# Neighbourhood attention: sixteen border stores spread over later steps and two queues

## The chip, the cores and the metric

The kernel runs on one core of one Trainium2 chip. The metric is the device time of one execution in microseconds (us). Runs of the same kernel are summed up by their median.

## The reference

The input is an image of 224 x 224 pixels with 192 channels (bf16). Each pixel attends to a 7 x 7 neighbourhood with dilation 2: the neighbours of one pixel all have its row parity and its column parity, and near the border the window is shifted inwards, not cut.

```python
q, k, v = split(x @ wqkv)                       # 192 channels each
r0 = clip(row - 6, 0, 224 - 13); c0 = clip(col - 6, 0, 224 - 13)
neighbours = (r0 + 0,2,..,12) x (c0 + 0,2,..,12)  # 49 pixels
p = softmax(q . k[neighbours] * 192**-0.5)
out = (p @ v[neighbours]) @ wo
```

## The kernel before, in words

**Tiles and steps.** Rows of one parity `rc` are taken eight at a time (`BR`), so the image makes 28 steps, listed in `seq` (L491): step 0 and step 1 work on even rows, then odd and even rows alternate. The loop over steps is at L522 with index `si`. A step has T = 7 rounds `t`, and in every round TensorE computes one group of scores (`s_group`, L399 and L400), which ScalarE turns into exponentials (L403). The query side of the next step is prepared in rounds 0 to 2 (`g_piece`, L343 and L351; evacuated by ScalarE and VectorE, L355 to L365), and edge columns are prepared by `edge_item` (L287, then VectorE's copies L295) and copied into place by `edge_copies`, half of them on GpSimd (POOL, L322 and L323).

**Values.** `y_unit` (L405) multiplies the exponentials with the input itself: for each column tile n it reads the key block in `XN[rc]`, which holds 14 tiles of 128 rows, in two halves that take turns as the steps advance down the image. The plan `yplan` (L379) says in which round each of the four units of a step begins; units of a step reach into rounds 0 and 1 of the next step. The unit of round 2 (cc = 0, h = 1) reads tiles 7 to 13, in that order; that of round 4 (cc = 0, h = 0) starts with tile 0.

**Output.** In rounds 3 to 6 the products of the step before are finished: `o_mm` (L436) applies the folded output weights, VectorE divides by the sums (L440, L451) and writes into the buffer `o_sb`, of which there are three in turn (L442). After round 6, `store` (L453) sends the finished buffer of the step before to memory from the SP queue (L596). For eight rows at a constant distance that is five transfers: one large one for the middle of the rows and four small ones for the sides. Step 0 has the image's upper border in it and its eight rows are not evenly spaced (1, 3, 5 and 0, 2, 4, 6, 8): it takes eight transfers of one row each and two times four small ones, sixteen in all.

**Loads.** In step `si` the key block that step `si` + 1 is the first to use is loaded into `XN` by fourteen transfers, one for each tile: tiles 12 and 11 from SP in round 0 (L570), tiles 10, 9 and 8 from POOL in round 0 (L571) and the remaining nine, 13 and then 7 down to 0, from POOL in round 1 (L573). A load waits until TensorE has read the old contents of its tile for the last time. The transposed loads `xt` (L91) are issued from SP in rounds 1 and 4. VectorE builds masks in round 2 of steps 1, 2, 3 and 8 (`masks`, L593; instructions at L187 and L188).

**What sets the order.** The schedule is manual: each engine and each queue works through its instructions in the order in which the program writes them. A transfer waits on its issuing queue, and everything behind it on that queue waits too. On SP, and likewise on POOL, a transfer also waits for the transfer eight before it on that queue to have landed.

Of the kernel before, what the change touches and what calls it, by code (L numbers as in the profile page):

```python
# [7 lines left out]
BF = mybir.dt.bfloat16  # L8
# [14 lines left out]
NO = 7  # L23
# [4 lines left out]
def kernel(  # L28
# [7 lines left out]
    nc = tc.nc  # L36
    B, H, W, C = x.shape
# [14 lines left out]
    work = ctx.enter_context(tc.tile_pool(name="work", bufs=3))  # L52
# [181 lines left out]
    for reg in (LO, HI, OLO, OHI):  # L234
        c0, cn, p0 = reg
        pool_, tag = ((ps_s, "s"), (ps_y, "y"))[reg in (OLO, OHI)]
# [27 lines left out]
    def key_copy(rc, m, cc, ea, eb):  # L264
        if not 0 <= m < NJ:
            return
        t, k0 = xt[m], 64 * (m % 2)
        v, d = "p r (n c) -> p r n c", DROW[cc]
        ea(out=XA[rc][:, cc, :, k0:k0 + 64].rearrange("p n (r c) -> p r n c", c=KC),  # L269
                       in_=t[:, 2 * cc, rc:16:2, :].rearrange(v, c=KC))  # L270
        eb(out=XB[cc][rc][d, :, k0:k0 + 64].rearrange("p n (r c) -> p r n c", c=KC),  # L271
                       in_=t[d, 1, rc:16:2, :].rearrange(v, c=KC))
# [25 lines left out]
    def step_rows(rc, j):  # L298
        if rc == 0:
            first = (0, 3, j - 1, 10) if j > 0 else (0, 3, 0, 1)  # L300
            return [first, (3, 5, j, 0)]
        last = (5, 3, j + 1, 1) if j < NJ - 1 else (5, 3, j, 10)
        return [(0, 5, j, 7), last]
# [122 lines left out]
    def o_mm(st, ns, ccs=(0, 1), home=None):  # L426

        if home is None:
            po = ps_go.tile([128, 4, 256], F32, name="po", tag="go")
        else:  # L430
            po = home[0].tile([128, 2, 256], F32, name="po" + home[1], tag=home[1])
        k = 0
        for n in ns:
            for cc in ccs:
                for kt in range(2):
                    nc.tensor.matmul(po[:, k, 0:C + 1], lhsT=st.ysb[cc][:, kt, n, :], rhs=WP[:, cc, kt, :],  # L436
                                     start=(kt == 0), stop=(kt == 1))
                k += 1
        rs = work.tile([128, 4, 1], F32, name="rs", tag="rs", bufs=4)
        nc.vector.reciprocal(out=rs[:, 0:k], in_=po[:, 0:k, C:C + 1])  # L440
        if st.o is None:
            st.o = work.tile([128, 2 * NO, C], BF, name="o_sb", tag="o_sb", bufs=3)  # L442
        t0, step = 2 * ns[0] + ccs[0], 3 - len(ccs)
        return po, rs, k, st.o[:, t0:t0 + step * (k - 1) + 1:step, :]

# [4 lines left out]
            return  # L450
        nc.vector.tensor_tensor(out=o, in0=po[:, 0:k, 0:C], in1=rs[:, 0:k].to_broadcast([128, k, C]), op=ALU.mult)  # L451

    def store(st, engs, parts=None, cols=None):  # L453

        o = st.o
        n0, n1 = cols or (0, NO)
        runs = _affine([16 * b + l0 + 2 * i for (r0, n_, b, l0) in step_rows(st.rc, st.j) for i in range(n_)])
        q = [0]

        def dma(**kw):  # L460
            engs[q[0] % len(engs)].dma_start(**kw)
            q[0] += 1
        for (i0, n_, d0, stp) in runs:
            rows = slice(d0, d0 + (n_ - 1) * stp + 1, stp)
            if parts is not None and cols is None:
                pass
            elif n_ == BR:
                dma(out=op[rows, 4:4 + 15 * NO, :].rearrange("r (i n) c -> i r (n c)", n=NO),
                    in_=o[BR:128].rearrange("p t c -> p (t c)"))
            else:  # L470
                for r in range(n_):
                    dma(out=op[d0 + r * stp, 4:4 + 15 * NO, :].rearrange("(i n) c -> i n c", n=NO)[:, n0:n1],
                        in_=o[BR + i0 + r:128:BR, 2 * n0:2 * n1].rearrange("p t c -> p (t c)"))
            ps = slice(i0, i0 + n_)

            side = [(op[rows, 3, :], o[ps, 12:14, :].rearrange("p t c -> p (t c)")),
                    (op[rows, 0:3, C:2 * C], o[ps, 0:6:2, :]),
                    (op[rows, 0:3, 0:C], o[ps, 6:12:2, :]),
                    (out[0][rows, W - 6:W, :], o[ps, 1:12:2, :])]
            for k in range(4) if parts is None else parts:  # L480
                dma(out=side[k][0], in_=side[k][1])
# [14 lines left out]
    for rc, j in seq:  # L496
        st = Step()
# [20 lines left out]
            y_unit(st, cc, h, kt, nc.scalar.copy if kt == 0 or (cc, h) == (1, 0) else nc.vector.tensor_copy)  # L518

    T = len(groups)  # L520
    PIECES = ((0, 1), (2, 3), (4, 5), (6,))
    for si, st in enumerate(steps):  # L522
        rc, j = st.rc, st.j
        prev = steps[si - 1] if si else None
        nxt = steps[si + 1] if si + 1 < len(steps) else None
        st.ysb = [work.tile([128, 2, NO, 128], BF, name=f"ysb{cc}", tag=f"ysb{cc}", bufs=2) for cc in range(2)]

        for (cc, h, ts) in yplan:
            for kt in range(2):
                pend.append((si * T + ts[kt] + (si == 0), st, cc, h, kt))  # L530
        up = None if si < 2 else (prev.rc, prev.j + 1 + prev.rc)
        if up:
            key_copy(*up, 0, nc.vector.tensor_copy, nc.vector.tensor_copy)
        for t in range(T):
            s_group(st, t)
            if t == (6 if si == 1 else 3) and rc == 0 and 2 <= j + 1 < NJ:
                edge_item(j + 1)
            if si == 0:
                if t == 0:
                    rest()  # L540
                    g_piece(0, 0, 2)
                    edge_item(0)
                    edge_copies(0, 0, nc.gpsimd)
                    load_xn(nc.gpsimd, 0, 1, DOWN[7:])
                    load_xn(nc.gpsimd, 1, 0, DOWN[:7])
                    load_xn(nc.gpsimd, 1, 1, DOWN[5:7])
                    load_xn(nc.gpsimd, 1, 0, DOWN[7:])
                    load_xn(nc.gpsimd, 1, 1, DOWN[7:])
                elif t == 1:
                    fold_wo()  # L550
                    masks(nc.vector, 2)
                    for cc in range(2):
                        onehots(nc.vector, cc, 1)
                        key_copy(1, 0, cc, nc.vector.tensor_copy, nc.vector.tensor_copy)
                elif t < 5:
                    g_piece(nxt.rc, nxt.j, t - 2)
                elif t == 5:
                    edge_item(1)
                    edge_copies(nxt.rc, nxt.j, nc.vector)
            elif t < 3 and nxt is not None:  # L560
                g_piece(nxt.rc, nxt.j, t)
            if prev is not None:
                tp_ = t - (3 if nxt is not None else 2)
                if 0 <= tp_ < 4:
                    o_out(*o_mm(prev, PIECES[tp_]))
            run_y(si * T + t)
            if t == (0 if si > 2 else 2) and si > 0 and nxt is not None:
                edge_copies(nxt.rc, nxt.j, nc.gpsimd if si > 1 else nc.vector)
            if up and t == 0:
                load_xn(nc.sync, *up, (12, 11))  # L570
                load_xn(nc.gpsimd, *up, (10, 9, 8))  # L571
            elif up and t == 1:
                load_xn(nc.gpsimd, *up, (13, 7, 6, 5, 4, 3, 2, 1, 0))  # L573
            if nxt is None and t == 4:
                store(prev, [nc.sync, nc.gpsimd], parts=(1,), cols=(0, 4))
            if nxt is None and t == 6:
                first = o_mm(st, (0, 1, 2, 3), (0,))
            if t == 5 and up:
                key_copy(*up, 1, nc.scalar.copy, nc.vector.tensor_copy)

            if si == 1 and t in (0, 2, 4, 5):
                load_xt(3, (0, 2, 4, 5).index(t))
            elif si > 1 and t in (1, 4):
                load_xt(j + (4 if rc else 2), 2 * (rc == 0) + (t == 4))
            if si == 0 and t in (4, 5):
                key_copy(0, 1, t - 4, nc.vector.tensor_copy, nc.vector.tensor_copy)
            if si == 1:
                if t == 1:
                    grp_copy(nc.scalar.copy, 1)
                if t in (3, 5):  # L590
                    key_copy(1, 1, (t - 3) // 2, (nc.vector.tensor_copy, nc.scalar.copy)[(t - 3) // 2], nc.vector.tensor_copy)
            if t == 2 and si in (1, 2, 3, 8):
                masks(nc.vector, {1: 1, 2: 4, 3: 3, 8: 5}[si])  # L593
        if prev is not None:
            if nxt is not None:
                store(prev, [nc.sync])  # L596
            else:
                store(prev, [nc.sync, nc.gpsimd], parts=(0, 2, 3), cols=(4, NO))

    last = steps[-1]  # L600
    run_y((len(steps) - 1) * T + 7)
    second = o_mm(last, (4, 5, 6), (0,))
    run_y(10 ** 9)
    o_out(*first)
# [56 lines left out]
```

## Time and profile before

| what | value |
|---|---|
| time, median of 3 runs | 331.78 us (331.6 to 335.15) |
| the profiled execution: its span, the only time given for it | 332.4 us |
| TensorE busy | 314.8 us, 95% of the span |
| VectorE, ScalarE, GpSimd busy | 81%, 75%, 64% of the span |
| loads of key tiles, POOL | 332, of 48 KB, landing 4.4 us after issue in the median |
| loads of key tiles, SP | 60, of 48 KB |
| stores of one step, SP | 25 of 630 KB, and small ones |
| stores of single border rows, SP | 8 of 78.8 KB |

In the profile, PE is TensorE's matmuls, PEld its weight loads, DVE VectorE, ACT ScalarE, POOL GpSimd, and SPq the queue of the sync engine, whose rows are the times in which it issues transfers. A row of a time line has the start, the length, the engine, the line of the kernel, what is written from what, the number of instructions, and in brackets the idle time before it with what ended it. The span is the time between the first and the last recorded instruction, so it is not quite the device time of a run.

### The profile page before, as it was taken

Reading aid. Unit: us, or ns where it says so; the run is one execution under the profiler, and the core shown is the slowest. Engines: PE = TensorE matmul, PEld = TensorE weight load, DVE = VectorE, ACT = ScalarE, POOL = GpSimd, SP = SyncE. Lnnn points to the kernel's source line nnn. Section 1 sums busy time; section 2 is a strip of 40 time slices with the busy share of each in tenths; the row PEclk is TensorE's granted clock in tenths of the full one; section 3 lists DMA queues with packets and bytes.
Section 4 is the critical chain, followed back from the end, with each engine's and each line's share of the span. In section 5 each row is a group of like instructions: output and inputs, shape, how many; then the busy total and the mean of one; then the engine's idle time right before and its main releaser. Section 6 shows DMA issues by size and latency. Waiting matters only on the chain.

```text
span 332.4 us, 12183 instructions
## 1 busy us (share of the span) xinstructions
PE 314.8 (95%) x4948; PEld 273.2 (82%) x4948; DVE 269.1 (81%) x538; ACT 249.9 (75%) x525; POOL 212.5 (64%) x438
## 2 busy tenths in 40 slices
PE   7999899599999999999999999999999999999980
PEld 4557887588988889888998889888898889988980
DVE  7757989489888998889888898889888898887771
ACT  5648678298887877897877878788887988888652
POOL 2887668546677667675676666686677666753072
PEclk9999999799999999999999999999999999999997
DMA  9999995988899998999889987999989944545233
GB/s 165 179 188 168 191 181 149 173 178 202 215 208 213 180 192 202 216 211 172 186 214 213 161 216 179 188 227 199 183 206 227 204 110 127 162 127 130 46 106 103
DMA packets 106391, 58.98 MB, mean 177 GB/s; under 512 B 93008, under 2 KB 100184, under 8 KB 106336
## 3 DMA queue, kind: packets, MB, share of 16 engines
q1 hardware_dynamic: 89010, 40.82, 64.2%
q0 software_dynamic: 16416, 16.74, 20.9%
q8 instruction: 38, 0.62, 0.8%
q10 hardware_dynamic: 910, 0.66, 0.8%
q14 instruction: 17, 0.14, 0.2%
HBM read 19.56 MB, written 19.27 MB: 117 GB/s over the span
## 4 chain that ended last, share of the span: by engine, by line
PE 73%; DMA 12%; POOL 5%; DVE 4%; issue 2%; SPq 1%; ACT 1%; POOLq 0%; DVEq 0%; ACTq 0%
PE y L418 19%; PE po L436 18%; PE pg L343 13%; DMA xn<-in_x_dram 10%; PE s_ps L399 9%; PE s_ps L400 9%; POOL xn L103 4%; PE pg L351 3%; DVE o_sb L451 2%; DMA xt<-in_x_dram 1%; PE pe L287 1%; SPq L91 1%; DVE ysb L424 1%; ACT ysb L424 1%; DVE rs L440 0%
## 5 line engine op out<-in xcount | busy, mean ns | idle before, releaser
L103 POOL DMA_DIRECT2D xn<-in_x_dram x332 | 185.9, 589 | 86.5 <-PE y L418 49.7
L403 ACT ACTIVATE p_sb<-s_ps 128x448 bf16<-128x448 f32 (+3 forms) x196 | 105.6, 539 | 21.6 <-PE s_ps L400 21.1
L418 PE MATMUL y<-p_sb,xn 128*128 128x112 bf16 (+5 forms) x1736 | 108.5, 207 | 4.8 <-DMA xn<-in_x_dram 3.9
L418 PEld LDWEIGHTS <-xn 128*128 128x128 bf16 (+1 forms) x1736 | 95.7, 97 | 18.1 <-issue 7.3
L424 ACT CAST ysb<-y 128x504 bf16<-128x504 f32 (+1 forms) x140 | 73.3, 544 | 38.7 <-PE y L418 35.4
L400 PE MATMUL s_ps<-gb,xb 128*128 128x112 bf16 (+4 forms) x812 | 99.9, 212 | 0.3 <-ACT gb L357 0.3
L399 PE MATMUL s_ps<-ga,xa 128*128 128x112 bf16 (+4 forms) x812 | 100.1, 212 | 0.0
L451 DVE TENSOR_TENSOR o_sb<-po,rs 128x768 bf16<-128x768 f32 x109 | 93.6, 858 | 5.6 <-DMA out_dram<-o_sb 0.4
L436 PE MATMUL po<-WP,ysb 128*128 128x193 bf16 x770 | 84.6, 249 | 1.2 <-DVE o_sb L451 0.5
L400 PEld LDWEIGHTS <-xb 128*128 128x128 bf16 (+1 forms) x812 | 77.2, 99 | 0.0
L399 PEld LDWEIGHTS <-xa 128*128 128x128 bf16 (+1 forms) x812 | 73.8, 99 | 1.9 <-issue 1.3
L343 PE MATMUL pg<-xt,aw 128*128 128x327 bf16 (+5 forms) x420 | 69.0, 297 | 1.3 <-DMA xt<-in_x_dram 0.4
L436 PEld LDWEIGHTS <-ysb 128*128 128x128 bf16 x784 | 64.3, 98 | 2.7 <-ACT ysb L424 1.1
L424 DVE CAST ysb<-y 128x392 bf16<-128x392 f32 (+1 forms) x84 | 49.7, 592 | 0.7 <-PE y L418 0.6
L343 PEld LDWEIGHTS <-aw 128*128 128x128 bf16 x420 | 31.2, 100 | 14.4 <-issue 1.2
L440 DVE RECIPROCAL rs<-po 128x4 f32<-128x4 f32 x110 | 19.4, 177 | 23.2 <-PE po L436 21.7
L357 DVE CAST gb<-pg 64x872 bf16<-64x872 f32 x27 | 28.6, 1058 | 7.2 <-PE pg L351 6.6
L355 ACT CAST ga<-pg 128x872 bf16<-128x872 f32 x28 | 24.8, 886 | 8.7 <-PE pg L343 8.7
L360 DVE CAST gb<-pg 64x848 bf16<-64x848 f32 x27 | 28.2, 1044 | 0.4
L365 ACT CAST ga<-pg 128x848 bf16<-128x848 f32 x28 | 24.2, 866 | 0.6 <-PE pg L343 0.3
L271 DVE COPY xb<-xt 64x896 bf16<-64x896 bf16 x56 | 22.9, 409 | 0.8
L269 ACT COPY xa<-xt 128x896 bf16<-128x896 bf16 x25 | 23.5, 940 | 0.0
(81 smaller groups left out, 152.0 us busy)
## 6 DMA issues: line engine op xcount, KB each, us to landing
xn<-in_x_dram POOLq DMA_DIRECT2D x332, 48.0 KB, 4.4
out_dram<-o_sb SPq DMA_DIRECT2D x25, 630.0 KB
xn<-in_x_dram SPq DMA_DIRECT2D x60, 48.0 KB
xt<-in_x_dram SPq DMA_TRANSPOSE x56
out_dram<-o_sb SPq DMA_DIRECT2D x50, 9.0 KB
out_dram<-o_sb SPq DMA_DIRECT2D x8, 78.8 KB
out_dram<-o_sb SPq DMA_DIRECT2D x25, 18.0 KB
out_dram<-o_sb SPq DMA_DIRECT2D x26, 6.0 KB
```

The costliest lines, as they stand in the source:

```text
L103: eng.dma_start(out=XN[rc][p0:p0 + 64, XP * n + 64:XP * (n + 1)], in_=xp[r0:r0 + 15:2, KC * n:KC * (n + 1), :])
L343: nc.tensor.matmul(pg[:, a_:b_, 0:nq], lhsT=AW[w], rhs=xt[b][:, k, la:la + 2 * (b_ - a_ - 1) + 1:2, q0:q0 + nq], start=(a_ == ra if kind = ...
L355: nc.scalar.copy(out=A[0][:, 3:S, :], in_=pg[:, :, 0:nq].rearrange(v))
L357: mid(out=Bt[0][0:64, 3:S, :], in_=pg[0:64, :, 0:nq].rearrange(v))
L360: mid(out=Bt[1][64:128, HALO:S, :], in_=pg[64:128, :, 3:nq].rearrange(v))
L399: nc.tensor.matmul(o, lhsT=XA[rc][:, cc, n, 0:kn], rhs=a[:, lo:hi, :].rearrange(f), start=True, stop=False)
L400: nc.tensor.matmul(o, lhsT=XB[cc][rc][:, n, 0:kn], rhs=b_[:, lo:hi, :].rearrange(f), start=False, stop=True)
L403: nc.scalar.activation(out=p[0:kn, 0:off], in_=s_ps[0:kn, 0:off], func=ACTF.Exp)
L418: nc.tensor.matmul(y[:, BR * (a_ - h0):BR * (b_ - h0)], lhsT=XN[st.rc][kp, d:d + 128], rhs=p[kp, off + BR * (a_ - lo):off + BR * (b_ - lo) ...
L424: eng(out=o, in_=y[:, 0:BR * (h1 - h0)].rearrange("p (i n r) -> p i n r", n=NO, r=BR))
L436: nc.tensor.matmul(po[:, k, 0:C + 1], lhsT=st.ysb[cc][:, kt, n, :], rhs=WP[:, cc, kt, :], start=(kt == 0), stop=(kt == 1))
L451: nc.vector.tensor_tensor(out=o, in0=po[:, 0:k, 0:C], in1=rs[:, 0:k].to_broadcast([128, k, C]), op=ALU.mult)
```

## The change

The sixteen stores of step 0 are no longer issued at the end of step 1. `store` is called with a list and only writes them down (`held`). From step 2 on, one of them is taken from the list in each of the rounds 1, 2, 3, 5 and 6: in rounds 2 and 5 it is issued from SP, in rounds 1, 3 and 6 from POOL, in each case behind what the round issues on that queue anyway. Five go out in each of steps 2, 3 and 4, and the last one in round 1 of step 5, from POOL; SP gets six and POOL ten. The stores of the other steps stay where they are. There are four `o_sb` buffers instead of three. What is computed, and which bytes are stored, does not change.

```diff
-            st.o = work.tile([128, 2 * NO, C], BF, name="o_sb", tag="o_sb", bufs=3)
+            st.o = work.tile([128, 2 * NO, C], BF, name="o_sb", tag="o_sb", bufs=4)
...
-    def store(st, engs, parts=None, cols=None):
+    def store(st, engs, parts=None, cols=None, later=None):
...
         def dma(**kw):
+            if later is not None:
+                later.append(kw)
+                return
             engs[q[0] % len(engs)].dma_start(**kw)
             q[0] += 1
...
+    held = []
...
+            if si > 1 and held and t in (1, 2, 3, 5, 6):
+                (nc.sync if t in (2, 5) else nc.gpsimd).dma_start(**held.pop(0))
             if t == 2 and si in (1, 2, 3, 8):
                 masks(nc.vector, {1: 1, 2: 4, 3: 3, 8: 5}[si])
         if prev is not None:
-            if nxt is not None:
+            if si == 1:
+                store(prev, None, later=held)
+            elif nxt is not None:
                 store(prev, [nc.sync])
```

## The prediction

> **What bounds the kernel now.** I read the page first (engine shares, then the forty slices), then the time line of PE around the slice that stands out, then those of SP and POOL for what it waited for, then VectorE's, and the table by stage for prices. The steps of the main loop are called by their index `si`.
>
> ```profile
> PE 314.8 (95%) x4948; PEld 273.2 (82%) x4948; DVE 269.1 (81%) x538; ACT 249.9 (75%) x525; POOL 212.5 (64%) x438
> PE   7999899599999999999999999999999999999980
> PEclk9999999799999999999999999999999999999997
> DMA  9999995988899998999889987999989944545233
> ```
>
> PE is the bound, 95% of 332.4 us. Between the start and the tail one slice of 8.3 us sticks out: PE at 5, and the clock granted in it at 7. The share of the DMA engines falls to 5 in the slice before.
>
> ```profile
> 57.27 0.34 PE L418 MATMUL y<-p_sb,xn 128*128 128x56 bf16 x4
> 61.55 0.30 PE L418 MATMUL y<-p_sb,xn 128*128 128x112 bf16 x3 [3.94 <-DMA xn<-in_x_dram]
> 62.71 1.47 PE L436 MATMUL po<-WP,ysb 128*128 128x193 bf16 x8
> 65.28 0.88 PE L436 MATMUL po<-WP,ysb 128*128 128x193 bf16 x8
> ```
>
> This is step 3, t = 2. `y_unit` walks the key tiles n = 7, 8, ... 13; four matmuls run and the fifth, n = 11, waits 3.94 us for its load. Afterwards eight L436 matmuls take 1.47 us where later ones take 0.88: the clock has dropped too.
>
> ```profile
> 35.92 10.41 SPq L91 DMA_TRANSPOSE xt<-in_x_dram  x4
> 46.46 11.05 SPq L461 DMA_DIRECT2D out_dram<-o_sb  x16
> 57.62 1.42 SPq L103 DMA_DIRECT2D xn<-in_x_dram  x2
> 59.14 3.83 SPq L91 DMA_TRANSPOSE xt<-in_x_dram  x2
> ```
>
> Tiles 12 and 11 are the only two that step 2 loads from SP (L570). They stand in SP's order behind the sixteen stores of step 0's output, and leave at 57.62 to 59.04, just when PE wants them.
>
> ```profile
> 53.10 0.57 POOL L103 DMA_DIRECT2D xn<-in_x_dram  x1 [0.20 <-issue]
> 54.98 6.85 POOL L103 DMA_DIRECT2D xn<-in_x_dram  x12
> 70.56 1.67 POOL L103 DMA_DIRECT2D xn<-in_x_dram  x3 [6.76 <-PE y L418]
> ```
>
> POOL issues the other twelve tiles of step 2, the last (tile 0) at 53.10, then step 3's. Before 70.56 it waits 6.76 us for PE, so it has room there.
>
> ```profile
> 42.33:52.60 10.27, 10.27 (x170) 9.22 (x170) 9.25 (x19) 8.06 (x17) 6.44 (x13) 1.00 1.04 193
> 52.60:69.18 16.58, 12.45 (x185) 11.02 (x183) 11.23 (x23) 8.70 (x18) 9.61 (x22) 0.90 0.74 160
> 69.18:79.48 10.30, 10.30 (x173) 9.21 (x170) 8.64 (x17) 8.68 (x20) 6.55 (x12) 1.00 0.87 202
> 79.48:90.21 10.73, 10.73 (x186) 9.63 (x184) 9.22 (x19) 8.71 (x20) 8.12 (x19) 1.00 0.94 204
> 111.25:132.90 21.65, 21.47 (x354) 18.93 (x352) 19.71 (x39) 17.08 (x35) 15.15 (x32) 1.00 0.98 201
> ```
>
> The table by stage (length; then busy time of PE, PEld, DVE, ACT, POOL; clock; DMA share) cuts at the first L343 group of steps 2, 3, 4, 5, and of 8 with 9. Step 3 lasts 16.58 us; step 5, of the same kind, 10.73. The excess is 16.58 - 10.73 = **5.85 us**: 3.94 of waiting, the rest mostly lost clock.
>
> **The change part by part.** *Sixteen stores leave SP between 46.46 and 57.51.* The two loads then stand right behind the transposes and can leave at 46.46; what else they wait for, PE's last reads of these tiles in step 2's t = 0, was over by 44 (POOL's own loads with that wait left at 43.85). The landing time of POOL's loads of the same shape is 4.4 us in the median, 7.9 at most: tile 11, the second to leave, lands by 46.46 + 0.7 + 7.9 = 55.1 at worst, and PE wants it at 57.3. The wait goes with its clock loss: -5.85 us.
>
> *SP's later work.* SP's order becomes, in step 2: loads 1.42, transpose 1.9, store 0.7, transpose 1.9, a small store, then step 1's five stores, which must wait for VectorE's last o_sb write (54.35 before). So those start at 54.4 instead of 63.06, and step 3's two loads leave near 59.2 instead of 67.80. With step 4 now starting at 63.3 (69.18 - 5.85), they are wanted at 63.3 + 4.4 + 0.2 = 67.9; landing by 59.2 + 1.3 + 4.4 = 64.9 leaves 3.0 us. Six of the sixteen stores come back on SP over steps 2 to 4, two per step, 1.4 us at most. Cost 0, covered by these 3 us; without that cover it is their excess.
>
> *POOL gets ten stores*: three each in steps 2, 3 and 4, one in step 5, each behind or between its loads and edge copies (L322, L323). The only stores it issues before, in the tail (L461 on POOL), take 542 ns in the median, its loads 573: I take 0.57, so 1.7 us per step. Step 2's first store delays the edge copies from 53.72 to 54.3; the score group that needs them comes 4.7 into the step, at 57.3. Three stores delay step 3's twelve loads from 54.98 to about 56.7, their last from 61.3 to 63.0, landing near 67.4; the use is 63.3 + 7.56 = 70.9 (7.56 is from 79.48 to 87.04 in step 5). Three more go ahead of step 4's loads: 6 x 0.57 = 3.4 us, of which the 6.76 us wait above, shrunk by 5.85, takes 0.9; so 2.5 us later against PE. The last of these left 9.85 after step 4's start before (79.03), now 12.35, lands at 16.75 and is wanted at 10.30 + 7.56 = 17.86. Cost 0, but the cover is only 1.1 us. VectorE's `ge` copies wait for POOL's edge copies as well: in step 5 these ran from 0.15 us into the step before (79.63); behind step 4's loads and stores they run from 12.35 + 0.57 + 1.71 - 10.30 = 4.3 to 5.4, and the `ge` copy comes at 5.7 (85.20).
>
> *What is late next: tile 0 in step 3.* It left POOL at 53.10 and is wanted at 52.60 + 7.56 = 60.16 (in the run before, the stall gave it more time). It lands at 57.5 by the median, 61.0 by the longest row. The transposes that now run from 47.9 slow POOL too: with four of them on SP its loads came every 0.75 us (14 in 10.5 us) instead of 0.57, and eight such loads lose 1.4. So 0 to 61.0 + 1.4 - 60.16 = 2.2 us. A gain is excluded, as only lateness can arise here. I take 0.3, as the median row is nearest.
>
> *What is late next: VectorE in step 3.* It builds a mask there (L187 and L188, 57.64 to 59.37, 1.73 us), which lay under the stall. Lower end 0 (step 2 has the same mask and is 10.27 long), upper 1.73. Step 8 with its mask is the row that shows a price: 21.65 - (10.30 + 10.73) = 0.62 for the pair. But step 8 has an idle 1.25 us on VectorE ahead of L440 that a step of step 3's kind lacks. I take 1.0.
>
> *Fourth buffer.* Step 0's buffer is read until step 5, and in the changed program's order step 3 takes the new buffer and step 4's write waits for step 1's five stores, so nothing waits for the held ones. It can save the one 0.4 us wait of L451 for a store: between 0 and -0.4; I take 0, since that wait is on VectorE.
>
> *Sum*: -5.85 + 0.3 + 1.0 = -4.55, so 332.4 - 4.55 = 327.85 by the span of the profiled execution. The median of the runs, 331.78, stands 0.6 below that span, which gives **327.2 us**.
>
> **A rule against it.** SP's sixteen stores take 11.05 us, 0.69 each, while the DMA engines are half idle: the slice before the stall shows 5. The Trainium skill, DMA: Bandwidth & Descriptors, section Issuing engines are not separate DMA queues, says that all issuing engines share the same 16 DMA engines and that spreading only saves issue time, usually small against the transfer. By that rule the sum would be 0 and the time 331.8; the trace does not agree here, since 0.69 us of issue stands beside half-idle engines.
>
> **The rivals.** *A, the stall goes (above)*: 327.2; its own range runs from no cost at all, 332.4 - 5.85 - 0.6 = 325.95, to the whole mask and the longest landing, 1.73 + 0.84 more, 328.5.
>
> *B, the wait moves to POOL's tiles*: tile 0 in step 3 late by the full 2.2, one more microsecond from step 4's or 5's thin cover, and the mask's 1.0: 332.4 - 5.85 + 2.2 + 1.0 + 1.0 - 0.6 = 330.15. For it: landing times of 7.5 us on the chain of waits while transposes run. Against: the DMA engines had half of 52 to 61 us free.
>
> *C, transfers and not issue set the time*: the same bytes move, tile 11 lands as late as before, 331.8. Against: the half-empty slice.
>
> *D, POOL falls behind, slower*: the place is tile 0 of steps 4 and 5, behind six and nine held stores; it decides once POOL runs more than 3.6 us later against PE than before (2.5 forecast; 17.86 - 9.85 - 4.4 = 3.6). If a store costs POOL's longest row for a load, 0.842, and landing takes 7.9, the lag is 6 x 0.842 - 0.9 = 4.2 plus 3.5, so 4.1 us beyond the cover, a stall like the present one; such a stall costs 5.85. One leaves 333.1, two give 332.4 - 4.55 + 11.7 - 0.6 = 338.9. Against: its median landing and 542 ns a store.
>
> **How the numbers follow.** A 0.71, B 0.17, C 0.05, D 0.07. The prediction is A's 327.2. The range reaches from A's lower end less the 0.4 of the buffer, 325.6, into B, 330.5; outside lie C, D and the end of B, near 0.17. One per cent, about what a measurement can tell from no change, is 3.3 us: faster (below 328.5) is A, 0.71; B and C are within, 0.22; D is slower, 0.07.
>
> **What would show it.** Right: no wait of PE for an xn load near 57 us, granted clock 1.00 through step 3, SP's two loads near 46.5, step 3 at 11 to 12 us, steps 4 to 6 as long as before. B shows as a PE wait for xn near 60, behind POOL; D as such waits in steps 4 and 5, with POOL's idle time before L103 gone; C as tile 11 still late although it left early. The forecast is wrong if step 3 stays over 14 us or a later step grows by more than 1.

## The result and the profile after

| | kernel before | kernel after |
|---|---|---|
| time, median of 6 runs each | 331.74 us (331.27 to 335.15) | 327.66 us (326.37 to 328.64) |
| profiled execution: span | 332.4 us | 325.3 us (its own time 328.23) |

The ratio is 0.9849, with a 95% interval of 0.9815 to 0.9882: 1.5% faster, against a forecast of 327.2 us.

The page of after, the same four rows:

```profile
PE 310.4 (95%) x4948; PEld 270.2 (83%) x4948; DVE 268.8 (83%) x538; ACT 249.6 (77%) x525; POOL 218.1 (67%) x448
PE   7899899999999999999999999999999999999980
PEclk9999999999999999999999999999999999999996
DMA  8999999999998999799989999999998943654233
```

The slice in which PE stood at 5 and its clock at 7 has no counterpart: between the start and the tail nothing is below 8. The low DMA slice ahead of it is gone as well. POOL has ten instructions more (448 for 438), the ten stores, and 5.6 us more of busy time.

The time line of PE in after, at t = 4 of step 2 and t = 2 of step 3:

```profile
47.87 0.54 PE L418 MATMUL y<-p_sb,xn 128*128 128x112 bf16 x8 [0.54 <-DMA xn<-in_x_dram]
...
55.43 0.47 PE L418 MATMUL y<-p_sb,xn 128*128 128x56 bf16 x7
```

At 55.43 all seven tiles go through in one group of seven. Before, this group broke off after four and waited 3.94 us. The 0.54 us at 47.87 is a wait that was not forecast: a tile of the opening loads, in step 2.

The time line of SP in after:

```profile
44.12 1.31 SPq L103 DMA_DIRECT2D xn<-in_x_dram  x2
45.54 1.63 SPq L91 DMA_TRANSPOSE xt<-in_x_dram  x1
47.26 1.17 SPq L597 DMA_DIRECT2D out_dram<-o_sb  x1
48.48 1.64 SPq L91 DMA_TRANSPOSE xt<-in_x_dram  x1
50.17 0.47 SPq L597 DMA_DIRECT2D out_dram<-o_sb  x1
52.53 4.78 SPq L464 DMA_DIRECT2D out_dram<-o_sb  x5
57.43 1.39 SPq L103 DMA_DIRECT2D xn<-in_x_dram  x2
```

The two loads of tiles 12 and 11 leave at 44.12, 11.3 us ahead of the group that reads them. The two held stores of step 2 (L597) take 1.17 us for a whole row and 0.47 for a small one; the four of steps 3 and 4 take 0.89 to 0.91 and 0.45 to 0.48.

The time line of POOL in after, around the stores of steps 2 and 4 (POOL issues them while TensorE is in steps 3 and 5):

```profile
52.94 0.53 POOL L597 DMA_DIRECT2D out_dram<-o_sb  x1 [0.70 <-DVE o_sb L451]
...
53.93 1.13 POOL L597 DMA_DIRECT2D out_dram<-o_sb  x2
...
55.52 7.29 POOL L103 DMA_DIRECT2D xn<-in_x_dram  x12
...
75.32 1.70 POOL L597 DMA_DIRECT2D out_dram<-o_sb  x3
```

In these groups a store takes 0.53 to 0.57 us; all ten together have 0.60 in the median and 0.88 at most. The table by stage, cut at the first L343 group of steps 2, 3, 4, 5 and 6 (length; busy time of PE, PEld, DVE, ACT, POOL; clock; DMA share, GB/s):

```profile
40.10:51.05 10.95, 10.41 (x170) 9.16 (x171) 9.59 (x19) 8.03 (x17) 9.05 (x17) 1.00 1.27 207
51.05:61.90 10.85, 10.85 (x186) 9.64 (x182) 10.45 (x23) 8.52 (x18) 9.55 (x20) 1.00 0.93 200
61.90:72.36 10.46, 10.40 (x173) 9.21 (x170) 8.83 (x17) 8.69 (x20) 7.24 (x16) 1.00 1.09 195
72.36:83.24 10.88, 10.88 (x185) 9.58 (x183) 9.21 (x19) 8.70 (x20) 9.62 (x20) 1.00 1.00 206
```

Step 3 went from 16.58 to 10.85 us and kept its clock (1.00 for 0.90). Steps 2 to 5 together take 43.14 us, where they took 10.27 + 16.58 + 10.30 + 10.73 = 47.88: **4.74 us less**.

**Reading the two spans.** They differ by 7.1 us, more than the change gave. 2.23 us of that arise before step 2, which begins at 42.33 in before and at 40.10 in after, although both programs are alike up to there: the opening of before's profiled execution was a long one (in the fourteen kept profiles step 2 begins at 39.75 to 43.96 us). So these profiles are compared by the lengths of steps, not by spans. The profiled executions of e1 and e8 below were long ones of their kernels, which the ratios leave out; they serve only to show where a wait stands and what it costs its step.

### The profile page after: what moved, and what is told of

The parts are those of the page before. It is cut to its first block, busy times and chain, and to the rows that moved or that the text cites. A ratio compares the mean times of both kernels' runs of the same rounds, so it can differ in the third digit from the quotient of the medians.

```text
span 325.3 us, 12180 instructions
## 1 busy us (share of the span) xinstructions
PE 310.4 (95%) x4948; PEld 270.2 (83%) x4948; DVE 268.8 (83%) x538; ACT 249.6 (77%) x525; POOL 218.1 (67%) x448
## 4 chain that ended last, share of the span: by engine, by line
PE 69%; DMA 11%; DVE 7%; POOL 5%; issue 3%; SPq 1%; ACT 1%; POOLq 0%; DVEq 0%; ACTq 0%
PE y L418 19%; PE po L436 16%; PE pg L343 13%; DMA xn<-in_x_dram 10%; PE s_ps L399 9%; PE s_ps L400 9%; POOL xn L103 5%; PE pg L351 3%; DVE o_sb L451 3%; DMA xt<-in_x_dram 2%; DVE ysb L424 1%; SPq L91 1%; PE pe L287 1%; DVE gb L357 1%; DVE gb L360 1%
## 5 line engine op out<-in xcount | busy, mean ns | idle before, releaser
L400 PE MATMUL s_ps<-gb,xb 128*128 128x112 bf16 (+4 forms) x812 | 98.6, 210 | 0.4 <-ACT gb L357 0.3
L399 PE MATMUL s_ps<-ga,xa 128*128 128x112 bf16 (+4 forms) x812 | 98.9, 210 | 0.0
L400 PEld LDWEIGHTS <-xb 128*128 128x128 bf16 (+1 forms) x812 | 76.2, 98 | 0.0
L399 PEld LDWEIGHTS <-xa 128*128 128x128 bf16 (+1 forms) x812 | 72.9, 98 | 1.6 <-issue 0.8
L343 PE MATMUL pg<-xt,aw 128*128 128x327 bf16 (+5 forms) x420 | 68.0, 294 | 1.4 <-DMA xt<-in_x_dram 0.8
L343 PEld LDWEIGHTS <-aw 128*128 128x128 bf16 x420 | 31.0, 99 | 14.1 <-issue 1.5
## 6 DMA issues: line engine op xcount, KB each, us to landing
out_dram<-o_sb POOLq DMA_DIRECT2D x5, 78.8 KB, 5.8
```

Of the source, the lines that this page charges most:

```text
L343: nc.tensor.matmul(pg[:, a_:b_, 0:nq], lhsT=AW[w], rhs=xt[b][:, k, la:la + 2 * (b_ - a_ - 1) + 1:2, q0:q0 + nq], start=(a_ == ra if kind = ...
L399: nc.tensor.matmul(o, lhsT=XA[rc][:, cc, n, 0:kn], rhs=a[:, lo:hi, :].rearrange(f), start=True, stop=False)
L400: nc.tensor.matmul(o, lhsT=XB[cc][rc][:, n, 0:kn], rhs=b_[:, lo:hi, :].rearrange(f), start=False, stop=True)
```

## The experiments

The theory: the 16 stores hold SP for the time it takes to *issue* them, the two loads stand behind them in order, and PE's wait with its clock loss is all there is to gain. Rivals: the DMA engines are what is short (C of the prediction); the fourth buffer does the work; any one queue would do as well. Each experiment's times and the kernel before's come from the same chip. Lengths of steps are by the table by stage; undisturbed, steps 2, 4, 6 take 10.3 us and steps 3, 5, 7 take 10.7.

### Is it the order on SP? (e1_loads_first)

Before, with the sixteen stores kept together on SP, but issued in round 0 of step 2 behind its two loads, no longer at the end of step 1.

```diff
+                if si == 2:
+                    store(steps[0], [nc.sync])
...
-            if nxt is not None:
+            if si == 1:
+                pass
+            elif nxt is not None:
```

> The kernel before with one change: the two SP loads of step 2 stand ahead of the sixteen stores, which all stay on SP, right behind them. Theory (SP is late as a queue, 11 us of issuing have to go somewhere): step 3 falls from 16.58 to about 10.9 us, but step 3's own two loads then leave SP near 67.8 as before, while step 4, starting near 63.4, wants them at 67.9; they land near 71.5, so step 4 waits some 3.5 us and grows from 10.3 to 14 or 16 us. Time 329.5 to 331.7. Rival (only the order of these two loads mattered, spreading is not needed): step 4 stays at 10.3, time 327 to 328.

334.05 us against 334.45, ratio 0.9986 (0.9943 to 1.0029). Its time line of SP, then its PE:

```profile
46.41 1.31 SPq L103 DMA_DIRECT2D xn<-in_x_dram  x2
47.81 11.34 SPq L461 DMA_DIRECT2D out_dram<-o_sb  x16
...
67.91 1.40 SPq L103 DMA_DIRECT2D xn<-in_x_dram  x2
```

```profile
72.49 0.42 PE L418 MATMUL y<-p_sb,xn 128*128 128x112 bf16 x3 [4.61 <-DMA xn<-in_x_dram]
```

PE stands still for the same tiles as before, but one step on: step 3 is down to 11.05 us, and the loads of step 3 now leave at 67.91 behind the stores, so step 4 takes 17.93 us, more than the 14 to 16 expected. The stall belongs to whichever two loads stand behind the sixteen stores. Moving them in one piece only hands it on.

### Is it issue time or bytes? (e5_few_bytes)

Before, with the eight row stores of step 0 cut to one seventh of their bytes; the rest of these rows is left out.

```diff
-                    dma(out=op[d0 + r * stp, 4:4 + 15 * NO, :].rearrange("(i n) c -> i n c", n=NO)[:, n0:n1],
-                        in_=o[BR + i0 + r:128:BR, 2 * n0:2 * n1].rearrange("p t c -> p (t c)"))
+                    n2 = 1 if st.first else n1
+                    dma(out=op[d0 + r * stp, 4:4 + 15 * NO, :].rearrange("(i n) c -> i n c", n=NO)[:, n0:n2],
+                        in_=o[BR + i0 + r:128:BR, 2 * n0:2 * n2].rearrange("p t c -> p (t c)"))
```

> The kernel before, but each of the eight row stores of step 0 writes only one seventh of its columns (768 bytes from each of 15 partitions instead of 5376); the rest of these eight rows is left out of the output. The number of transfers and of their pieces is the same. Theory (issue time on SP): the sixteen stores still take 10 to 11 us on SP, tile 11 is as late, step 3 stays near 16 us, time 331 to 332. Rival (moving the bytes sets it): the sixteen stores take under 7 us, the wait of step 3 is under 1 us, time near 327.5.

334.28 us against 334.45, ratio 1.0006 (0.996 to 1.0051). Its SP, then three microseconds in the middle of the stores from its table by stage:

```profile
45.90 11.37 SPq L461 DMA_DIRECT2D out_dram<-o_sb  x16
57.39 1.42 SPq L103 DMA_DIRECT2D xn<-in_x_dram  x2
```

```profile
52.00:55.00 3.00, 2.82 (x49) 2.15 (x48) 2.86 (x7) 2.04 (x5) 1.87 (x3) 1.00 0.19 45
```

With a seventh of the bytes in the eight row stores the sixteen still take 11.37 us (11.05 before) while the DMA engines are busy 0.19 of the time, and PE waits 4.42 us. So bytes are not what holds SP. Waiting for earlier transfers to land is not it either: instruction by instruction in before's trace, 9.3 of the 11.05 us are the issues themselves, and the only two pauses over 0.1 us, ahead of the eighth and the ninth store, make 1.2 us together.

### How long is the wait per store? (e6_hold_two)

After's code, three buffers; fourteen stores stay at the end of step 1 and two follow on SP in step 3.

```diff
-            if si > 1 and held and t in (1, 2, 3, 5, 6):
-                (nc.sync if t in (2, 5) else nc.gpsimd).dma_start(**held.pop(0))
+            if si == 3 and held and t in (2, 5):
+                nc.sync.dma_start(**held.pop(0))
...
+                for kw in held[2:]:
+                    nc.sync.dma_start(**kw)
+                del held[2:]
```

> The kernel before, with two of the eight row stores held and issued from SP in rounds 2 and 5 of step 3; fourteen stores stay at the end of step 1. Theory (issue time adds up store by store): the two loads leave some 1.8 us earlier, the wait falls from 3.94 to about 2.1 us. If a wait of that length leaves the granted clock at 1.00, step 3 is 10.85 + 2.1 = 13 us and the time 328.2; if the clock falls as before, step 3 is near 14.9 and the time 330. Rival (all or nothing: the loads wait for the landing of the stores and not for their issue): the wait stays above 3 us.

333.89 us against 334.45, ratio 0.9947 (0.9904 to 0.9991); step 3 takes 15.62 us. The wait was 3.30 us, where 2.1 was expected, and so over the 3 us by which the rival was to be known. SP's rows speak against the rival all the same: the loads leave 0.12 us after the last of the fourteen issues.

```profile
44.80 9.31 SPq L604 DMA_DIRECT2D out_dram<-o_sb  x14
54.23 1.44 SPq L103 DMA_DIRECT2D xn<-in_x_dram  x2
```

They follow the first store by 9.43 us, instead of 11.16 before, and leave 3.39 us earlier in all (54.23 for 57.62). But PE began step 2 2.58 us earlier than in before's profile (39.75 for 42.33), so it came for the tile earlier too, and 3.94 - 3.39 + 2.58 = 3.13 us of the wait remain. The wait is the difference of two timetables, SP's issuing and PE's progress, and both shift with the opening (here SP's first store by 1.66 us, 44.80 for 46.46, and step 2 by 2.58). Steps 6 and 7 of e6 also wait for SP's tiles, 0.89 and 0.94 us; what is behind that stays open.

### The fourth buffer (e2_four_buffers, e3_three_buffers)

Before with `bufs=4`, and after with `bufs=3`; nothing else is changed.

> The kernel before with four output buffers instead of three, nothing else. Theory: no wait of weight goes, 331.7 within the scatter, step 3 stays at 16.6 us. Rival (the buffer carries part of the gain by itself): 330 or less.

> The changed kernel with three output buffers instead of four. Theory (steps 3 to 5 take the buffers of steps 1, 2, 3, whose stores leave SP a whole step before they are wanted, so the fourth buffer is not needed): no wait of VectorE's L451 for a store over 0.5 us, ratio to the kernel before as for the changed kernel, 0.985. Rival (with one buffer held only two are left, and VectorE waits for stores): one to two us more in each of steps 4 to 6, ratio 0.99 to 1.0.

e2: 332.99 us against 334.45, ratio 0.9956 (0.9916 to 0.9996). e3: 328.75 against 333.37, ratio 0.986 (0.9781 to 0.9939), and r_after, the changed kernel again on the same chip, 327.36, ratio 0.9816 (0.9719 to 0.9913). The PE of e2 and its step 3:

```profile
59.03 0.42 PE L418 MATMUL y<-p_sb,xn 128*128 128x112 bf16 x3 [2.70 <-DMA xn<-in_x_dram]
```

```profile
51.32:66.41 15.09, 12.21 (x183) 10.77 (x182) 11.36 (x23) 8.63 (x18) 7.89 (x17) 0.89 0.83 164
```

With the buffer alone the stall stays. The upper bound of e2's interval lies just under 1, so a small gain by the buffer is not excluded by the times, nor can it be told from the scatter of the stall's length. Without the buffer steps 2 to 9 of e3 agree with those of r_after within 0.02 us (step 3: 11.39 and 11.39, where 10.85 was expected of r_after). The buffer is not needed; the difference of 1.4 us between the two medians lies inside both intervals.

> The changed kernel once more, on the chip on which the next three run. Ratio to the kernel before 0.985, step 3 near 10.85 us, VectorE's ge copy waiting 1 us for POOL in step 5.

### One queue or two? (e4_sp_alone, e9_pool_alone)

After, with all sixteen on SP (e4), or all on POOL (e9), at the same places.

```diff
-                (nc.sync if t in (2, 5) else nc.gpsimd).dma_start(**held.pop(0))
+                nc.sync.dma_start(**held.pop(0))
...
+                nc.gpsimd.dma_start(**held.pop(0))
```

> The changed kernel with all sixteen held stores on SP. Theory (SP's issue time is the scarce thing; five more stores of 0.7 us on its 9.7 make 13.2 us in a step of 10.5): steps 3 and 4 are free, SP falls some 3 us behind in steps 3 and 4, and TensorE waits again for tiles 12 and 11 in steps 5 and 6, together about 3 us with 1 to 3 us of clock loss, ratio 0.99 to 1.0. Rival (spreading alone does it, the second queue is not needed): no wait over 0.6 us, ratio 0.985.

> The changed kernel with all sixteen held stores on POOL. Theory (POOL's queue has 2 to 3 us of room per step and 2.9 us of stores fill it): steps 3 and 4 as in the changed kernel, 11.4 and 10.5; POOL's edge copies for step 6 come over 1 us later, so VectorE waits 1 to 2.5 us for them in step 5, and tile 0 is late by up to 2.5 us in step 6; the two steps grow by 1 to 4 us in all, ratio 0.985 to 0.995. Rival (room on POOL is ample): steps 5 and 6 stay at 10.73 and 10.32.

e4: 329.41 us against 333.37, ratio 0.9868 (0.9799 to 0.9937). e9: 329.39 against 332.96, ratio 0.9924 (0.9883 to 0.9965); r_after2 beside it 327.82, ratio 0.9864 (0.9815 to 0.9913). PE's only wait for a load in the steps that follow, first of e4, then of e9:

```profile
101.34 0.30 PE L418 MATMUL y<-p_sb,xn 128*128 128x112 bf16 x3 [0.49 <-DMA xn<-in_x_dram]
```

```profile
92.98 0.54 PE L418 MATMUL y<-p_sb,xn 128*128 128x112 bf16 x8 [0.63 <-DMA xn<-in_x_dram]
```

e4 missed its expectation of about 3 us of waits in steps 5 and 6: SP alone loses 0.6 us in step 7 and 0.2 in step 6. POOL alone loses 0.8 in step 6 and 0.1 in step 7, less than the 1 to 4 expected. In the trace, then, two queues are worth under 1 us here. e9's interval overlaps r_after2's only at its lower end, so POOL alone may be a little slower; e4 can't be told from after. What counts is the spreading over steps.

> The changed kernel once more, as the yardstick for e10_masks_moved on the same chip. Ratio 0.982 to 0.986; step 3 between 10.85 and 11.4 us.

### What sets the pace of step 3 now? (e7_mask_twice, e10_masks_moved)

e7: after, with step 3's mask built a second time. e10: the held stores go out in steps 22 to 25 on SP, and the masks of steps 3 and 8 are moved to steps 0 and 24. The first lines are e7's, the others e10's.

```diff
+                if si == 3:
+                    masks(nc.vector, 3)
...
-            if si > 1 and held and t in (1, 2, 3, 5, 6):
-                (nc.sync if t in (2, 5) else nc.gpsimd).dma_start(**held.pop(0))
-            if t == 2 and si in (1, 2, 3, 8):
-                masks(nc.vector, {1: 1, 2: 4, 3: 3, 8: 5}[si])
+            if si > 21 and held and t in (1, 2, 3, 5, 6):
+                nc.sync.dma_start(**held.pop(0))
+            if (si, t) in ((0, 6), (1, 2), (2, 2), (24, 2)):
+                masks(nc.vector, {0: 3, 1: 1, 2: 4, 24: 5}[si])
```

> The changed kernel with the mask that VectorE builds in step 3 written twice (1.7 us more of VectorE work there, same values). Theory (without the long wait VectorE sets the pace of step 3, and its mask now costs TensorE about 0.66 us, the part of 1.73 that finds no idle VectorE time): step 3 grows from 11.39 by nearly the whole 1.7, to about 13 us. Rival (VectorE has room there, the 0.66 us come from POOL's stores): under 12 us.

> The stores held late as in e8_hold_late, and two masks moved to where VectorE has idle time: that of step 3 into round 6 of step 0, that of step 8 into round 2 of step 24. Theory: step 3 falls from 11.39 to about 10.75, step 4 from 10.46 to 10.31, steps 8 and 9 together from 21.63 to 21.05; 1.4 us less than the changed kernel in the main loop, ratio to the kernel before some 0.004 below that of r_after2. Rival (the masks cost their time wherever they stand): the start grows by 1 us or more and the sum is unchanged.

e7: 330.68 us against 332.96, ratio 0.9934 (0.9895 to 0.9974). Its PE, and the same group in r_after:

```profile
60.34 0.86 PE L436 MATMUL po<-WP,ysb 128*128 128x193 bf16 x8 [2.14 <-DVE ge L295]
```

```profile
57.87 0.85 PE L436 MATMUL po<-WP,ysb 128*128 128x193 bf16 x8 [0.23 <-DVE ge L295]
```

PE's wait for VectorE's copy, behind the mask in its order, grew from 0.23 to 2.14 us, and step 3 from 11.39 to 13.24: the mask's whole 1.73 us and a little more (the medians differ by 330.68 - 327.82 = 2.9, with intervals that overlap). One mask still mostly fits beside PE, a second does not.

e10: 328.58 us against 332.96, ratio 0.9881 (0.9843 to 0.992). Its step 3 takes 10.72 us, step 4 10.32 and steps 8 and 9 together 21.09 (21.61 in r_after): some 1.3 us less, as expected. But the mask moved to step 24 costs its time there. Steps 24 and 25 take 10.60 us each, where they take 10.31 in e8, in after and in r_after; step 24 of e10:

```profile
274.82:285.42 10.60, 10.60 (x173) 9.29 (x170) 10.27 (x21) 8.64 (x18) 7.30 (x16) 1.00 0.55 152
```

So step 8's mask, in line with the rival, only moved its price: 0.5 us saved, 0.6 paid. Step 3's mask, moved into the opening, shows no price there: it stands at 27.90 to 29.58 us, and from the wait of the opening for POOL's edge copy (0.97 us in e10, ending at 20.61; 0.52 in r_after, ending at 20.20) to step 2 both take 19.91 us. That wait lies ahead of the moved mask, so it is not the mask's. Neither is the wait of 2.53 us in step 2:

```profile
50.30 0.54 PE L418 MATMUL y<-p_sb,xn 128*128 128x112 bf16 x8 [2.53 <-DMA xn<-in_x_dram]
```

The profiled execution of e8 below, with its masks in place, waits there for 2.89. By the lengths of steps some 0.7 us of the 1.3 would remain; the medians, 328.58 against r_after2's 327.82, do not show it.

### Does it matter when they go? (e8_hold_late)

After, with the sixteen on SP in steps 22 to 25.

```diff
-            if si > 1 and held and t in (1, 2, 3, 5, 6):
-                (nc.sync if t in (2, 5) else nc.gpsimd).dma_start(**held.pop(0))
+            if si > 21 and held and t in (1, 2, 3, 5, 6):
+                nc.sync.dma_start(**held.pop(0))
```

> The changed kernel with the held stores issued from SP alone in steps 22 to 25, where no transposed loads are left, instead of on two queues in steps 2 to 5. Theory (what counts is that the stores leave SP's crowded part; POOL's ten stores cost a little in steps 4 and 5): step 3 near 10.85, steps 4 and 5 at 10.30 and 10.73 as in the kernel before instead of 10.46 and 10.88, no ge wait for POOL, the end of the kernel unchanged; 0.3 us faster than the changed kernel, ratio 0.984. Rival (late stores collide with the last steps): steps 22 to 26 grow by 1 us or more in total and the ratio is 0.987 or more.

329.03 us against 333.37, ratio 0.9845 (0.9765 to 0.9924). Steps 4 and 5 take 10.47 and 10.72, so step 4 did not return to 10.30 and the ten stores on POOL are not what lengthens it; steps 22 to 25 take their usual 10.3 and 10.7. No version tried is measurably faster than after.

## Why the prediction was right, and where its terms were off

**The stall, -5.85.** Right, place and size. Step 3 lost 16.58 - 10.85 = 5.73 us, SP's loads left right behind the transposes (44.12, with a start 2.2 us earlier than before's; forecast 46.46), and the clock stayed at 1.00. e1 and e5 show the cause: sixteen issues in a row on one queue, with loads behind them. The size is that of one execution, though. In the kernels that leave the sixteen stores ahead of step 2's loads, step 3 exceeds 10.73 by 5.85 (before), 4.36 (e2) and 7.30 (e5).

**SP's later work and POOL's ten stores, 0.** Right to 0.15 us. Step 1's stores started at 52.53 and step 3's loads at 57.43; the forecast's 54.4 and 59.2 less the earlier start of 2.2 are 52.2 and 57.0. POOL took 0.60 us a store in the median; 0.57 was forecast. The cover of 1.1 us, which the text gave for the last tile loaded in step 4, was used up in after: that load left 12.88 us into step 4 (12.35 forecast) and landed 5.24 us later (4.4 forecast), just too late for step 5, where TensorE's weight load waits for it. POOL had itself waited there for a held store to land:

```profile
72.55 2.83 POOL L103 DMA_DIRECT2D xn<-in_x_dram  x5 [0.62 <-DMA out_dram<-o_sb]
80.06 0.41 PEld L418 LDWEIGHTS <-xn 128*128 128x128 bf16 x8 [0.21 <-DMA xn<-in_x_dram]
```

It cost 0.15 us (step 5 takes 10.88 for 10.73); r_after and r_after2 have no such wait and take 10.73. VectorE's `ge` copy in step 5 lost nothing: POOL's edge copies were done 5.67 us into the step, and the copy came at 5.72, in after as in before and in r_after.

**Tile 0 in step 3, +0.3.** It did not come: no wait near there in after or in r_after.

**VectorE's mask in step 3, +1.0.** Right in kind (e7, e10), too large. Step 3 exceeds 10.73 by 0.12 in after, 0.66 in r_after and 0.54 in r_after2. The first may be small because PE had just waited 0.54 us in step 2, which gave VectorE time to catch up; that is not shown, for e1 and e8, which wait there for 1.19 and 2.89 us, still have 0.32 and 0.31. The backlog also reaches into step 4, 10.46 for 10.30, and is gone there in e10 (10.32).

**Not forecast: the opening's loads in step 2.** PE waits for a tile of the opening's loads for 0.54 us in after, 1.19 in e1, 2.53 in e10, 2.89 in e8, and for no more than 0.1 us in the other ten profiles. In the kernel before, an early PE only waits longer at the stall, as e6 shows, which hides what the opening won or lost. Without the stall nothing behind it does.

**The sum.** Steps 2 to 5 changed by -4.74 us in after's profile (r_after -5.07, r_after2 -4.91), against -4.55. That after's profile agrees so closely is in part luck: the mask and tile 0 cost 0.12 us in step 3 where 1.3 were forecast, and what was put at nothing, step 2's wait (0.68), step 4's backlog (0.16) and step 5 (0.15), came to 0.99. The medians differ by 331.74 - 327.66 = 4.08, and by 6.0 and 5.1 where r_after and r_after2 ran beside the kernel before. The term that was wrong without harm is the step from span to time: the median was set 0.6 below the span. In the thirteen profiled executions whose time is known the time lies 1.8 to 3.5 us *above* the span, so the 332.4 span of before belongs to a time near 335, most likely its slowest run of 335.15.

**The rivals.** C did not occur: tile 11 left early and was there in time, and e5 shows that the bytes do not hold SP. B and D did not occur as waits that weigh; step 5's 0.15 us is a wait of D's kind. The sentence of the Trainium skill (DMA: Bandwidth & Descriptors, Issuing engines are not separate DMA queues) that issue time is usually small against the transfer holds here for one store, not for the queue: POOL's held stores took 0.60 us to issue and landed 5.7 us after the issue began (medians in after), but sixteen issues in order on SP took 11.05. That more issuing engines bring little beyond issue time is in line with e4, where SP alone was within 0.8 us of two queues by the trace.

## What to carry to other kernels

When a load comes late, look at what its queue was doing just before: many small transfers in one piece cost their number times the issue time (0.7 us in the mean here), however few their bytes. Spread them over steps in which the queue has gaps; moved in one piece, they take the stall along. Look again, too, at what is moved to another place for a gain, as with the mask of step 8: its price may be waiting there. And take the profiled execution's own place among the runs before taking prices in absolute time from it.

## What the runs showed of the hardware

**A short idle time costs itself, a longer one the clock too.** PE's waits and what the step took beyond its usual length, one execution each:

| wait, us | 0.49 | 0.54 | 0.63 | 0.89 | 1.19 | 2.53 | 2.70 | 2.89 | 3.30 | 3.94 | 4.42 | 4.61 |
|---|---|---|---|---|---|---|---|---|---|---|---|---|
| excess of the step, us | 0.62 | 0.68 | 0.80 | 1.06 | 1.33 | 2.68 | 4.36 | 4.64 | 4.89 | 5.85 | 7.30 | 7.63 |
| clock at 0.50 for, us | 0 | 0 | 0 | 0 | 0 | 0 | 3.41 | 3.41 | 3.41 | 3.41 | 6.83 | 6.83 |
| run | e4 | after, step 2 | e9 | e6, step 6 | e1, step 2 | e10 | e2 | e8 | e6, step 3 | before | e5 | e1, step 4 |

Up to 2.53 us the wait costs 0.1 to 0.2 more than itself, and the clock granted in the step is 1.00. From 2.70 us on it costs 1.6 to 3.0 more, and the clock granted is 0.89 in e2's step 3 (above). The 0.89 is a mean: cut finer, the tables by stage show the clock at 0.50 for 3.41 us, or twice that, and at 1.00 again behind it. Before's, right behind the wait:

```profile
61.94:65.35 3.41, 3.41 (x45) 3.32 (x42) 1.57 (x5) 0.98 (x2) 0.73 (x4) 0.50 1.33 206
```

Half of the slow time in which PE works is the price. In before PE works through all 3.41 us, so 1.7 us are lost, of the 1.9 that the step took beyond its wait; in e5 the slow clock begins at 59.30, 1.30 us before the wait ends, and (6.83 - 1.30) / 2 = 2.8 us are lost, of 2.9.

The steps of e10 and e6, by their tables by stage:

```profile
40.52:53.47 12.95, 10.41 (x169) 9.16 (x170) 9.52 (x19) 8.02 (x17) 8.88 (x16) 1.00 1.19 188
```

```profile
50.01:65.63 15.62, 12.13 (x184) 10.70 (x182) 11.14 (x23) 8.69 (x18) 9.40 (x22) 0.89 0.80 164
```

PE's busy time is 10.41 us for the one, as in step 2 of after, and 12.13 for the other, for the same work that takes 10.85 in step 3 of after.

The Trainium skill, TensorE: Matmul & The Clock Gate, section HAM oscillation, warns of PE-idle gaps over some 3.4 us; here the clock fell already at waits of 2.70, 2.89 and 3.30. Where the limit lies is not shown, nor that the length alone decides. Within each trace the times at which the clock changes lie whole multiples of 3.41 us apart (before: 65.35 - 61.94 = 3.41, 61.94 - 24.39 = 37.55 = 11 x 3.413). Counted on from e10's own change at 15.35, its wait of 2.53 us lies across such a time, 1.71 us ahead of 49.48 and 0.82 behind it; of e2's 2.70 us, 2.24 lie ahead of 58.57, where the clock fell. A wait of 2.53 us that falls otherwise may cost the clock too.

**SP's issue time goes by the kind of transfer and hardly by its bytes.** Instruction by instruction in before's trace, the eight row stores of step 0 took 0.81 to 0.93 us each and the eight small ones 0.28 to 0.46. With a seventh of the bytes (e5) the row stores took 0.81 to 1.19, and the large store of a step, 630 KB against a row's 78.8, took 0.91 in after (median of 25). A key tile took 0.60 to 0.69 in these stretches. POOL's issue time is 0.60 in the median for the ten stores, of either size, and 0.59 in the mean for a key tile.
